# One SBUF tensor for keys and values, swapped key slots and fewer value loads at the end of a decode block

## The chip, the core and the metric

The kernel runs on one core of a Trainium2 chip. The metric is device time in microseconds (us), the median of timed runs. One more execution is recorded by the hardware profiler; all rows of the trace below are from that one.

## The reference

One decode step: two sequences (B = 2), one token each, D = 448, 16 heads of 256, a cache of 8192 positions, all in 32-bit floats.

```python
q = (layernorm(x) @ wq)                      # per head: 256
scores = einsum("bhqd,bhkd->bhqk", q, k_cache) * 256 ** -0.5
p = softmax(scores)
o = einsum("bhqk,bhkd->bhqd", p, v_cache)
h = x + o.reshape(B, 1, 4096) @ wo
h2 = h + ((ln(h) @ w_gate) * (ln(h) @ w_up)) @ w_down     # F = 1792
```

## The kernel before

There are 32 queries (head times sequence, `NQ`), numbered from 0 here. The keys of a query are 8 MB: on each of 128 partitions 64 rows (`NJ`) of 256 floats. Its values are the same size. Everything is read once.

**Engines.** VectorE makes the scores: a product of keys and query in place (`tensor_mul`), then a sum along each row (`tensor_reduce`), in two parts per query of 16 and 48 rows; the last two queries (`FINE`) in four parts of 16 rows. `top` takes the maximum over the free axis; `softmax` turns it on TensorE, takes the maximum again, and lets ScalarE make the exponentials. `mix` is the weighted sum of the values on TensorE, two rows at a time into four row groups of `o_ps`; `mixed` brings the four groups together (`o_sb`, `sel`, `oT`) and multiplies with `wo` once per head.

**Buffers.** `k_sb` is a ring of 112 rows: even queries' keys lie in rows 0 to 63, odd ones' in 48 to 111 (`k_base`). The 16 rows in common are scored first, so that the next load but one may start early. `v_sb` has 64 rows for values. Small tiles that live only at the start or the end are guests in `v_sb` (`guest`, `late_guest`).

**Order.** All large loads are issued by SyncE (SP) into one queue, in program order (the loop at line 612): values of query n-1, scores of query n, keys of query n+1. `Orders` notes who reads and writes which rows, and puts semaphore waits ahead of an instruction that needs them; an SP instruction that waits holds up all loads behind it. TensorE's part for queries 0 to `LOOP` - 1 is one loop in hardware (`turns`), the rest is straight code.

**The end.** `LATE` (line 25) cuts the values of the last four queries into nine loads, each of so many rows into its own place; `None` stands for the natural place in `v_sb`:

```python
LATE = (
    ((48, None), (16, None)),
    ((32, None), (32, None)),
    ((32, None), (32, ("k", 0))),
    ((16, ("k", 32)), (32, ("v", 32)), (16, ("v", 0))),
)
```

`EARLY` = `LOOP` = 28 is the first query of these. A query's second and later pieces are loaded behind the next keys (line 627), and summed after the next softmax (`late`, lines 621 to 624). `open_sums` (line 598) copies the sum of the other heads (`acc_ps`) and opens the last two accumulators with 16 small matmuls; for query 31 it stands ahead of the last piece of the sum (lines 641 to 645). Then come `last_head`, the second layernorm (its operand for TensorE is `xr`), the gate and up projections (`project`, `q_ps`) and the down projection (`down`, `y_ps`). The weights `wg`, `wu` and `wd` are loaded into the ring (`places`, line 660), behind the last values; `wd` in four loads.

Of the kernel before, what the change touches and what calls it, by code (L numbers as in the profile page):

```python
# [7 lines left out]
ALU = mybir.AluOpType  # L8
AX = mybir.AxisListType
# [3 lines left out]
P = 128  # L13
# [5 lines left out]
OVER = HC  # L19

AHEAD = 24
FIRST = ((NJ - AHEAD, NJ), (0, NJ - AHEAD))


LATE = (
    ((48, None), (16, None)),
    ((32, None), (32, None)),
    ((32, None), (32, ("k", 0))),
    ((16, ("k", 32)), (32, ("v", 32)), (16, ("v", 0))),
)  # L30
WQ, WO = 3 * 2 * DH + DH, 2 * D
WALL = 2 * WQ + 4 * WO
# [183 lines left out]
def decode_block(nc, x, k_cache, v_cache, w, wg, wu, wd, out):  # L216
# [3 lines left out]
    def sb(name, *shape):  # L220
        return nc.alloc_sbuf_tensor(name, list(shape), F32)[:]
# [20 lines left out]
        put("PE", "transpose", out, in_, ident[:n, :n], r=(*r, "ident"), w=w, mark=mark)  # L242

    sb("align", P, ALIGN)
    k_sb = sb("k_sb", P, 2 * NJ - OVER, DH)
    v_sb = sb("v_sb", P, NJ, DH)
    w_sb = sb("w_sb", P, WALL)
    buffers = {"k": k_sb, "v": v_sb}
    v_flat = v_sb.rearrange("p j d -> p (j d)")

    def guest(name, at, rows, *shape):

        n = 1
        for k in shape:
            n *= k
        o.homes[name] = ("v", at, n)
        got = v_flat[:rows, at : at + n]
        if len(shape) > 1:
            dims = "abc"[: len(shape)]
            got = got.rearrange(f"p ({' '.join(dims)}) -> p {' '.join(dims)}", **dict(zip(dims, shape)))  # L260
        return got
# [5 lines left out]
        h, b = divmod(i, B)  # L267
        return cache[b, h].rearrange("(p j) d -> p j d", p=P)[:, lo:hi, :]

    def load_keys(name, cache, i, lo, hi, buf, at, event=None):  # L270
        o.load(
            "SP", name, buffers[buf][:, at : at + hi - lo, :], keys(cache, i, lo, hi),
            writes=[(buf, at * DH, (at + hi - lo) * DH)], event=event,
        )

    def k_base(i):
        return i % 2 * (NJ - OVER)

    def load_k(i, lo=0, hi=NJ):
        load_keys(f"d_k_{i}_{lo}", k_cache, i, lo, hi, "k", k_base(i) + lo)  # L280

    def v_parts(i):
        got, lo = [], 0
        for n, place in LATE[i - EARLY] if i >= EARLY else ((NJ, None),):
            buf, at = place or ("v", lo)
            got.append((lo, lo + n, buf, at))
            lo += n
        return got

    def load_v(i, part):  # L290
        lo, hi, buf, at = part
        load_keys(f"d_v_{i}_{lo}", v_cache, i, lo, hi, buf, at, "e_v" if i < LOOP else None)

    def load_w(name, k, lo, hi, event=None):
        o.load("SP", name, w_sb[:, lo:hi], w[k][:, lo:hi], writes=[("w", lo, hi)], event=event)
# [5 lines left out]
        return 2 * WQ + h % 4 * WO  # L301

    load_w("d_w0", 0, 0, WQ)
    for lo, hi in FIRST:
        load_k(0, lo, hi)

    ident = sb("ident", P, P)
    put("POOL", "memset", ident, 0.0, w=["ident"])
# [134 lines left out]
    def score_parts(i):  # L443
        if i == 0:
            return list(FIRST)
        at = [(k - 1) % (NJ // HC) * HC if i % 2 == 0 else k * HC for k in range(NJ // HC)]
        if i in FINE:
            return [(lo, lo + HC) for lo in at]
        return [(at[0], at[0] + HC), (at[1], at[1] + NJ - HC)]

    def scores(i, part, between=None):
        h, b = divmod(i, B)
        s, name = s_t[i % 2], f"s{i % 2}"
        lo, hi = score_parts(i)[part]
        at = k_base(i) + lo
        kt = k_sb[:, at : at + hi - lo, :]
        qk, there = kt, ("k", at * DH, (at + hi - lo) * DH)
        if i == 0 and part == 0:
            qk, there = v_sb[:, : hi - lo, :], ("v", 0, (hi - lo) * DH)
        q, slot = qs[b], q_at(h)  # L460
        here = ("k", at * DH, (at + hi - lo) * DH)
        dve(
            "tensor_mul", qk, kt, q[:, slot, :][:, None, :].to_broadcast([P, hi - lo, DH]),
            r=[here, (f"q{b}", slot, slot + 1)], w=[there],
        )
        if between is not None:
            between()
        dve("tensor_reduce", s[:, lo:hi], qk, axis=AX.X, op=ALU.add, r=[there], w=[(name, lo, hi)])

    def top(i):  # L470
        dve("tensor_reduce", m, s_t[i % 2], axis=AX.X, op=ALU.max, r=[f"s{i % 2}"], w=["m"],
# [24 lines left out]
    def mix(i, parts):  # L496
        k = other(i)
        with common(i):
            take("e_v", i, 16)
            for lo, hi, buf, at in parts:  # L500
                for t in range(lo // 2, hi // 2):
                    g, j = 32 * (t % 4), at + 2 * t - lo
                    mm(
                        o_ps[k][g : g + 2, :], p_t[k][:, 2 * t : 2 * t + 2],
                        buffers[buf][:, j : j + 2, :], t < 4, t >= NJ // 2 - 4,
                        r=[f"p{k}", (buf, j * DH, (j + 2) * DH)], w=[f"o_ps{k}"],
                        mark="PE" if t == hi // 2 - 1 else None,
                    )

# [71 lines left out]
    def group(t, q):  # L581
        return t[:, q * YW : (q + 1) * YW]

    late_at = [HC * DH]

    def late_guest(name, rows, *shape):
        got = guest(name, late_at[0], rows, *shape)
        late_at[0] += o.homes[name][2]
        assert late_at[0] <= 2 * HC * DH
        return got  # L590

    h_sb = late_guest("h_sb", B, DC * P)
# [19 lines left out]
    for n in range(NQ + 1):  # L612
        hp, at = divmod(n, 2 * B)
        parts = v_parts(n - 1) if n > 0 else []
        if n > 0:
            load_v(n - 1, parts[0])
        if n < NQ:
            scores(n, 0, (lambda: softmax(n - 1)) if n > 0 else None)
        else:
            softmax(n - 1)  # L620
        if late is not None:
            mix(n - 2, late)
            mixed(n - 2)
            late = None
        if n + 1 < NQ:
            load_k(n + 1)
        for part in parts[1:]:
            load_v(n - 1, part)
        if n % 8 == 1:
            k = n // 8 + 1  # L630
            load_w(f"d_w_{k}", k, WQ if k == H // 4 else 0, WALL, event("e_w", n))
        def norm_last():
            if n > 0:
                norm(n - 1)

        if n == NQ:
            norm_last()
        else:
            for part in range(1, len(score_parts(n))):
                scores(n, part, norm_last if part == 1 else None)  # L640
        if n == NQ:
            mix(n - 1, parts[:-1])
            open_sums()
            mix(n - 1, parts[-1:])
            mixed(n - 1)
        elif n + 1 < NQ and len(parts) > 1:
            late = parts[1:]
            mix(n - 1, parts[:1])
        elif n > 0:
            mix(n - 1, parts)  # L650
            mixed(n - 1)
        if at == 2 and hp + 1 < H // 2:
            queries(n - 1, hp + 1)
        if n < NQ:
            if n == 0:
                o.ops["PE"].append(lambda: turns())
            top(n)

    k_flat = k_sb.rearrange("p j d -> p (j d)")
    places = {"wd": 0, "wg": (NJ - OVER) * DH, "wu": (NJ - OVER) * DH + NF * D}  # L660
    wd_t, wg_t, wu_t = (k_flat[:, places[n] :][:, : NF * D] for n in ("wd", "wg", "wu"))
    for name, t, src in (("wg", wg_t, wg), ("wu", wu_t, wu)):
        for k, half in enumerate(PIECES[name]):
            o.load("SP", f"d_{name}_{k}", t[:, half], src[:, half],
                   writes=[("k", places[name] + half.start, places[name] + half.stop)])
    at = 0
    for n in DOWN:
        o.load("SP", f"d_wd_{at}", wd_t[:, at * D : (at + n) * D], wd[:, at * D : (at + n) * D],
               writes=[("k", at * D, (at + n) * D)])
        at += n  # L670

    o.load(
# [6 lines left out]

    def project(out, out_name, t, name, k, between=None):  # L680
        wide, piece = WIDE[{"wg": "B_w_gate", "wu": "B_w_up"}[name]][k], PIECES[name][k]
        here = ("k", places[name] + piece.start, places[name] + piece.stop)
        t = t[:, piece]
        for c in range(DC):
            for g in range(4):
                xs = xr[:, c]
                if c < DC - 1:
                    at = c * sum(wide) + sum(wide[:g])
                else:
                    xs = xr[:, c + g % 2]  # L690
                    at = 3 * sum(wide) + (wide[0] if g >= 2 else 0)
                mm(
                    out[32 * g : 32 * g + 32, : wide[g]], xs.rearrange("p b r -> p (b r)"),
                    t[:, at : at + wide[g]], c == 0, c == DC - 1, r=["xr", here], w=[out_name],
                    mark="PE" if c == DC - 1 and g == 3 else None,
                )
            if c == 1 and between is not None:
                between()
# [54 lines left out]
    def down(lo, hi):  # L753
        for k in range(lo, hi):
            n, g = FF[k]
            for q in range(YN):
                mm(
                    y_ps[32 * q : 32 * q + 32, :], hmT[n // 2][:, n % 2, g, :],
                    wd_t[:, k * D + q * YW : k * D + (q + 1) * YW], False, k == NF - 1,
                    r=[f"hmT{n // 2}", ("k", k * D, (k + 1) * D)], w=["y_ps"],  # L760
                    mark="PE" if k == NF - 1 and q == YN - 1 else None,
                )

# [94 lines left out]
```

## Time and profile before

| | |
|---|---|
| median of 3 timed runs | 1301.37 us (1301.36 to 1301.38) |
| profiled execution, first to last instruction (span) | 1300.5 us |
| VectorE busy | 1130.8 us, 87% |
| TensorE matmuls busy | 488.8 us, 38% |
| ScalarE busy | 62.6 us, 5% |
| DMA: bytes read, mean rate | 561.19 MB, 432 GB/s |

The page gives no other time of the profiled execution than its span; the timed runs lie 0.87 us above it, which is what comes ahead of the first and behind the last instruction. Busy shares are averages over the whole span and say little about its end. Matmuls of 32-bit operands are done in two passes, so the trace counts twice as many as the program has; the rows that show the order of the program count each once.

### The profile page before, as it was taken

The page shows a single profiled execution, that of the slowest core. Times are in us where ns is not written, and L with a number is a line of the kernel's source. Part 1 is how long each engine was busy: PE and PEld are TensorE (multiplying, and loading weights), DVE is VectorE, ACT ScalarE, POOL GpSimd, SP SyncE. Part 2 cuts the span into 40 slices and gives each one's busy share as a digit, 9 for nine tenths or more (in the row PEclk, how much of TensorE's full clock was granted, in tenths as well). Part 3 has the DMA queues.
Part 4 walks back from the last instruction along what each step waited for, and adds up shares of the span by engine and source line. Part 5 has one row for each costly group of instructions (what it writes and reads, how often), then busy time and mean ns, then how long its engine had stood idle before and what let it go on. Part 6 is the DMA issues. An engine that isn't in the chain of part 4 may idle for free.

```text
span 1300.5 us, 6955 instructions
## 1 busy us (share of the span) xinstructions
PE 488.8 (38%) x2972; PEld 168.9 (13%) x2972; DVE 1130.8 (87%) x275; ACT 62.6 (5%) x184; POOL 1.4 (0%) x9
## 2 busy tenths in 40 slices
PE   3035422363331633215343063432424334243368
PEld 2011100120100201002101021010111001010113
DVE  7996988888988689888889868898888897889991
ACT  1000000000000000000000000000000000000000
POOL 0000000000000000000000000000000000000000
PEclk8566756686656766558666576665766667666578
DMA  9999999999999999999999999999999999999998
GB/s 414 423 434 448 424 437 431 427 441 423 448 424 435 448 423 443 427 439 429 435 435 423 433 448 423 448 424 443 427 443 427 423 436 445 426 438 429 435 433 374
DMA packets 12111, 561.45 MB, mean 432 GB/s; under 512 B 1602, under 2 KB 1732, under 8 KB 1988
## 3 DMA queue, kind: packets, MB, share of 16 engines
q1 hardware_dynamic: 12096, 561.30, 99.8%
q8 instruction: 6, 0.10, 0.0%
q14 instruction: 5, 0.04, 0.0%
q10 hardware_dynamic: 4, 0.00, 0.0%
HBM read 561.19 MB, written 0.11 MB: 432 GB/s over the span
## 4 chain that ended last, share of the span: by engine, by line
DMA 70%; DVE 29%; PE 0%; issue 0%; SPq 0%
DMA k_sb<-in_A_k_cache_dram 68%; DVE k_sb L229 14%; DVE s L229 14%; DMA k_sb<-in_wd_dram 2%; DVE nm L229 0%; PE y_ps L229 0%; SPq L176 0%; DVE m L229 0%; PE sm L229 0%; DVE v_sb L229 0%; DVE rl L229 0%
## 5 line engine op out<-in xcount | busy, mean ns | idle before, releaser
L229 DVE TENSOR_TENSOR k_sb<-k_sb,q 128x12288 f32<-128x12288 f32 (+2 forms) x67 | 549.6, 8203 | 130.3 <-DMA k_sb<-in_A_k_cache_dram 130.3
L229 DVE TENSOR_REDUCE s<-k_sb 128x48 f32<-128x12288 f32 (+2 forms) x67 | 549.3, 8198 | 0.2
L229 PE MATMUL o_ps<-v_sb,p 128*2 128x512 f32 x2000 | 288.2, 739 | 397.7 <-PEq L183 387.6
L229 PEld LDWEIGHTS o_ps<-v_sb,p 128*2 128x2 f32 x2000 | 53.7, 97 | 603.8 <-issue 591.3
L229 PE MATMUL sm<-nm,ones 1*128 1x1 f32 x64 | 16.6, 326 | 191.7 <-PEq L183 175.1
L229 PE MATMUL sm<-ident,m 128*1 128x128 f32 x32 | 10.9, 341 | 137.0 <-PEq L183 106.1
L229 PE MATMUL q_ps<-w_sb,xb 128*128 128x256 f32 (+1 forms) x172 | 59.3, 503 | 0.0
L229 ACT ACTIVATE o_sb<-o_ps 128x512 f32<-128x512 f32 x32 | 19.1, 597 | 703.9 <-PE o_ps L229 703.9
L229 PE MATMUL sm<-sel,o_sb 128*128 128x1 f32 x256 | 33.7, 253 | 25.8 <-PEq L183 22.9
L229 PE MATMUL acc_ps<-w_sb,oT 128*2 128x448 f32 x60 | 36.6, 749 | 15.9 <-PEq L183 11.0
L229 PEld LDWEIGHTS sm<-nm,ones 1*128 1x128 f32 x64 | 14.6, 283 | 201.2 <-issue 183.5
L229 PEld LDWEIGHTS sm<-sel,o_sb 128*128 128x128 f32 x256 | 31.8, 195 | 55.6 <-issue 48.2
L229 PEld LDWEIGHTS q_ps<-w_sb,xb 128*128 128x128 f32 x172 | 33.7, 200 | 30.0 <-issue 27.6
L229 PE MATMUL sm<-lsum,ones 128*128 128x1 f32 x64 | 17.5, 342 | 26.0 <-PEq L183 23.1
L229 ACT ACTIVATE nb<-sm 128x1 f32<-128x1 f32 x32 | 5.5, 171 | 395.7 <-PE sm L229 395.7
L229 PEld LDWEIGHTS sm<-ident,m 128*1 128x1 f32 x32 | 2.6, 81 | 149.8 <-issue 115.3
L229 PEld LDWEIGHTS sm<-lsum,ones 128*128 128x128 f32 x64 | 15.6, 303 | 28.0 <-issue 24.7
L229 ACT ACTIVATE q<-q_ps,rstd 128x512 f32<-128x512 f32 (+1 forms) x18 | 11.5, 640 | 71.9 <-PE q_ps L229 71.9
L229 PE MATMUL o_ps<-k_sb,p 128*2 128x512 f32 x48 | 9.3, 934 | 6.1 <-DMA k_sb<-in_A_v_cache_dram 6.1
L229 ACT ACTIVATE p<-s,nb 128x64 f32<-128x64 f32 x32 | 11.1, 347 | 1.0
L229 DVE TENSOR_TENSOR v_sb<-k_sb,q 128x6144 f32<-128x6144 f32 x1 | 6.6, 6557 | 4.8 <-DMA k_sb<-in_A_k_cache_dram 4.8
L229 PE MATMUL q_ps<-k_sb,xr 128*32 128x256 f32 (+3 forms) x96 | 10.0, 506 | 1.6 <-DMA k_sb<-in_B_w_gate_dram 1.6
(79 smaller groups left out, 85.1 us busy)
## 6 DMA issues: line engine op xcount, KB each, us to landing
v_sb<-in_A_v_cache_dram SPq DMA_DIRECT2D x4, 4096.0 KB, 30.5
w_sb<-in_w_dram SPq DMA_DIRECT2D x3, 3584.0 KB, 37.8
v_sb<-in_A_v_cache_dram SPq DMA_DIRECT2D x1, 6144.0 KB, 24.3
k_sb<-in_A_k_cache_dram SPq DMA_DIRECT2D x1, 5120.0 KB, 24.6
v_sb<-in_A_v_cache_dram SPq DMA_DIRECT2D x2, 2048.0 KB, 27.3
k_sb<-in_A_v_cache_dram SPq DMA_DIRECT2D x1, 4096.0 KB, 35.3
k_sb<-in_B_w_gate_dram SPq DMA_DIRECT2D x1, 3136.0 KB, 32.4
k_sb<-in_A_k_cache_dram SPq DMA_DIRECT2D x1, 3072.0 KB, 11.6
```

The costliest lines, as they stand in the source:

```text
L229: o.put(engine, lambda: f(*args, **kw), r, w, mark, event)
```

## The change

`k_sb` and `v_sb` become one tensor `c_sb` of 112 + 64 rows, and `RING` = 112 is the row at which the values' place begins. Even queries' keys now lie in the upper slot (rows 48 to 111), odd ones' in the lower. Query 0's first piece is its first 24 rows, loaded into the values' place and multiplied there. `LATE` has three entries: query 28 is an ordinary one, its values one load, its sum in TensorE's loop (`LOOP` = 29). A place in `LATE` is now a row of `c_sb`, so that a load may reach across the end of the ring. `wg` and `wu` lie at the ring's start, `wd` from row 84.

```diff
-FIRST = ((NJ - AHEAD, NJ), (0, NJ - AHEAD))
+FIRST = ((0, AHEAD), (AHEAD, NJ))
+RING = 2 * NJ - OVER
 LATE = (
-    ((48, None), (16, None)),
-    ((32, None), (32, None)),
-    ((32, None), (32, ("k", 0))),
-    ((16, ("k", 32)), (32, ("v", 32)), (16, ("v", 0))),
+    ((32, RING), (32, RING + 32)),
+    ((64, NJ),),
+    ((46, RING + 16), (18, NJ)),
 )
...
-    k_sb = sb("k_sb", P, 2 * NJ - OVER, DH)
-    v_sb = sb("v_sb", P, NJ, DH)
+    c_sb = sb("c_sb", P, RING + NJ, DH)
+    v_sb = c_sb[:, RING:, :]
...
     def k_base(i):
-        return i % 2 * (NJ - OVER)
+        return (1 - i % 2) * (NJ - OVER)
...
-    for lo, hi in FIRST:
-        load_k(0, lo, hi)
+    load_keys("d_k_first", k_cache, 0, *FIRST[0], RING)
+    load_k(0, *FIRST[1])
...
-        at = [(k - 1) % (NJ // HC) * HC if i % 2 == 0 else k * HC for k in range(NJ // HC)]
+        at = [(k - i % 2) % (NJ // HC) * HC for k in range(NJ // HC)]
...
         if n == NQ:
-            mix(n - 1, parts[:-1])
             open_sums()
-            mix(n - 1, parts[-1:])
+            mix(n - 1, parts)
             mixed(n - 1)
...
-    places = {"wd": 0, "wg": (NJ - OVER) * DH, "wu": (NJ - OVER) * DH + NF * D}
+    places = {"wg": 0, "wu": NF * D, "wd": (NJ + 20) * DH}
```

The order on SP, from the load of query 29's keys to the last values. Each row is a load into the tensor on the left of the arrow; the shape is partitions by floats (16384 is 64 rows, 4096 is 16). Before:

```order
L176 DMA k_sb<-in_A_k_cache_dram 128x16384 [waits DVE]
L176 DMA v_sb<-in_A_v_cache_dram 128x12288 [waits PE]
L176 DMA k_sb<-in_A_k_cache_dram 128x16384 [waits DVE]
L176 DMA v_sb<-in_A_v_cache_dram 128x4096
L176 DMA v_sb<-in_A_v_cache_dram 128x8192 [waits PE]
L176 DMA k_sb<-in_A_k_cache_dram 128x16384 [waits DVE]
L176 DMA v_sb<-in_A_v_cache_dram 128x8192 [waits PE] x2
L176 DMA k_sb<-in_A_v_cache_dram 128x8192 [waits DVE]
L176 DMA k_sb<-in_A_v_cache_dram 128x4096 [waits DVE]
L176 DMA v_sb<-in_A_v_cache_dram 128x8192 [waits PE]
L176 DMA v_sb<-in_A_v_cache_dram 128x4096 [waits PE]
```

And the same stretch now:

```order
L176 DMA c_sb<-in_A_k_cache_dram 128x16384 [waits DVE]
L176 DMA c_sb<-in_A_v_cache_dram 128x16384 [waits PE]
L176 DMA c_sb<-in_A_k_cache_dram 128x16384 [waits DVE]
L176 DMA c_sb<-in_A_v_cache_dram 128x8192 [waits PE]
L176 DMA c_sb<-in_A_k_cache_dram 128x16384 [waits DVE]
L176 DMA c_sb<-in_A_v_cache_dram 128x8192
L176 DMA c_sb<-in_A_v_cache_dram 128x16384 [waits DVE,PE]
L176 DMA c_sb<-in_A_v_cache_dram 128x11776 [waits PE]
L176 DMA c_sb<-in_A_v_cache_dram 128x4608 [waits PE]
```

All 64 rows of query 28's values now stand ahead of query 30's keys (the third row), where 48 stood before; query 30's values are one load that waits for VectorE and TensorE, and query 31's are two.

The order on TensorE, from the turned maximum of query 31 to the end of its weighted sum (`p` are the exponentials, `ident` and `pair` rows are those of `open_sums`). Before:

```order
L229 MATMUL sm<-ident,m 1x128 [waits DVE]
L229 MATMUL sm<-nm,ones 128x1 [waits ACT,DVE]
L229 MATMUL sm<-lsum,ones 128x1 [waits ACT]
L229 MATMUL o_ps<-k_sb,p 2x512 [waits d_v_31_0]
L229 MATMUL o_ps<-k_sb,p 2x512 x7
L229 MATMUL o_ps<-v_sb,p 2x512 [waits d_v_31_16]
L229 MATMUL o_ps<-v_sb,p 2x512 x15
L229 MATMUL o_ps<-v_sb,ident 2x128 [waits DVE]
L229 MATMUL o_ps<-v_sb,ident 2x128 x3
L229 MATMUL y_ps<-v_sb,pair 32x112 x4
L229 MATMUL o_ps<-v_sb,p 2x512 [waits d_v_31_48]
L229 MATMUL o_ps<-v_sb,p 2x512 x7
```

And now:

```order
L229 MATMUL sm<-ident,m 1x128 [waits DVE]
L229 MATMUL sm<-nm,ones 128x1 [waits ACT,DVE]
L229 MATMUL sm<-lsum,ones 128x1 [waits ACT]
L229 MATMUL o_ps<-c_sb,ident 2x128 [waits DVE]
L229 MATMUL o_ps<-c_sb,ident 2x128 x3
L229 MATMUL y_ps<-c_sb,pair 32x112 x4
L229 MATMUL o_ps<-c_sb,p 2x512 [waits d_v_31_0]
L229 MATMUL o_ps<-c_sb,p 2x512 x22
L229 MATMUL o_ps<-c_sb,p 2x512 [waits d_v_31_46]
L229 MATMUL o_ps<-c_sb,p 2x512 x8
```

The opening matmuls moved ahead of the whole sum, and the sum has two pieces, of 46 and 18 rows.

## Rows read from the trace of the kernel before

**Rows 1.** The page: chain by engine, the large queue, bytes.

```profile
DMA 70%; DVE 29%; PE 0%; issue 0%; SPq 0%
...
q1 hardware_dynamic: 12096, 561.30, 99.8%
...
HBM read 561.19 MB, written 0.11 MB: 432 GB/s over the span
```

**Rows 2.** The chain of waits in order of time: start us, us, what.

```profile
401.99 4.43 DVE k_sb L229
...
449.11 4.43 DVE k_sb L229
...
487.74 4.42 DVE k_sb L229
```

**Rows 3.** Timeline of SP: issues of query 30's and 31's keys, last store.

```profile
1168.39 0.33 SPq L176 DMA_DIRECT2D k_sb<-in_A_k_cache_dram  x1
...
1203.34 0.33 SPq L176 DMA_DIRECT2D k_sb<-in_A_k_cache_dram  x1
...
1298.87 0.34 SPq L176 DMA_DIRECT2D out_dram<-v_sb  x1
```

**Rows 4.** Timeline of VectorE at the end: start, us, operation, [idle before <-releaser].

```profile
1159.42 4.43 DVE L229 TENSOR_TENSOR k_sb<-k_sb,q 128x4096 f32<-128x4096 f32 x1 [3.58 <-DMA k_sb<-in_A_k_cache_dram]
...
1194.38 4.42 DVE L229 TENSOR_TENSOR k_sb<-k_sb,q 128x4096 f32<-128x4096 f32 x1
...
1203.24 4.40 DVE L229 TENSOR_TENSOR k_sb<-k_sb,q 128x4096 f32<-128x4096 f32 x1
...
1265.16 0.22 DVE L229 TENSOR_REDUCE m<-s 128x1 f32<-128x64 f32 x1
...
1268.20 0.72 DVE L229 COPY v_sb<-acc_ps 2x448 f32<-2x448 f32 x2
```

**Rows 5.** Timeline of TensorE: weighted sums of 64, 64, 32, 32 and 16 rows.

```profile
1101.58 9.83 PE L229 MATMUL o_ps<-v_sb,p 128*2 128x512 f32 x64 [12.74 <-PEq L183]
...
1140.22 9.29 PE L229 MATMUL o_ps<-v_sb,p 128*2 128x512 f32 x64 [12.73 <-PEq L183]
...
1207.80 6.20 PE L229 MATMUL o_ps<-v_sb,p 128*2 128x512 f32 x32 [0.75 <-DMA v_sb<-in_A_v_cache_dram]
...
1246.59 3.61 PE L229 MATMUL o_ps<-v_sb,p 128*2 128x512 f32 x32 [0.57 <-DMA v_sb<-in_A_v_cache_dram]
...
1268.01 3.40 PE L229 MATMUL o_ps<-k_sb,p 128*2 128x512 f32 x16
```

**Rows 6.** Timeline of what follows the last weighted sum.

```profile
1277.59 0.60 ACT L229 ACTIVATE o_sb<-o_ps 128x512 f32<-128x512 f32 x1 [10.15 <-PE o_ps L229]
...
1281.57 0.57 DVE L229 COPY xr<-sm 128x96 f32<-128x96 f32 x3 [0.74 <-PE sm L229]
...
1283.13 3.63 PE L229 MATMUL q_ps<-k_sb,xr 128*32 128x512 f32 x16 [1.60 <-DMA k_sb<-in_B_w_gate_dram]
...
1295.17 0.59 PE L229 MATMUL y_ps<-k_sb,v_sb 128*32 128x112 f32 x16
...
1296.47 2.03 PE L229 MATMUL y_ps<-k_sb,v_sb 128*32 128x112 f32 x64 [0.71 <-DMA k_sb<-in_wd_dram]
1298.10 0.16 PEld L229 LDWEIGHTS y_ps<-k_sb,v_sb 128*32 128x32 f32 x8 [0.22 <-DMA k_sb<-in_wd_dram]
```

**Rows 7.** Windows: stretch, length, busy by engine, granted clock (PEclk), DMA share, GB/s.

```profile
1282.00:1288.00 6.00, 4.87 (x24) 1.85 (x28) 1.44 (x9) 0.00 (x0) 0.00 (x0) 0.50 0.98 413
1288.00:1296.00 8.00, 7.75 (x148) 4.88 (x140) 1.86 (x5) 0.69 (x1) 0.00 (x0) 0.99 1.00 421
```

More of the change, by code (lines that the diff above doesn't have):

```diff
@@ L244, in decode_block @@
     sb("align", P, ALIGN)
-    k_sb = sb("k_sb", P, 2 * NJ - OVER, DH)
-    v_sb = sb("v_sb", P, NJ, DH)
+    c_sb = sb("c_sb", P, RING + NJ, DH)
+    v_sb = c_sb[:, RING:, :]
     w_sb = sb("w_sb", P, WALL)
-    buffers = {"k": k_sb, "v": v_sb}
-    v_flat = v_sb.rearrange("p j d -> p (j d)")
+    c_flat = c_sb.rearrange("p j d -> p (j d)")
     def guest(name, at, rows, *shape):
@@ L255, in guest @@
             n *= k
-        o.homes[name] = ("v", at, n)
-        got = v_flat[:rows, at : at + n]
+        at += RING * DH
+        o.homes[name] = ("c", at, n)
+        got = c_flat[:rows, at : at + n]
         if len(shape) > 1:
@@ L268, in keys, with rows, load_keys @@
         return cache[b, h].rearrange("(p j) d -> p j d", p=P)[:, lo:hi, :]
-    def load_keys(name, cache, i, lo, hi, buf, at, event=None):
+    def rows(at, n):
+        return ("c", at * DH, (at + n) * DH)
+    def load_keys(name, cache, i, lo, hi, at, event=None):
         o.load(
-            "SP", name, buffers[buf][:, at : at + hi - lo, :], keys(cache, i, lo, hi),
-            writes=[(buf, at * DH, (at + hi - lo) * DH)], event=event,
+            "SP", name, c_sb[:, at : at + hi - lo, :], keys(cache, i, lo, hi),
+            writes=[rows(at, hi - lo)], event=event,
         )
     def k_base(i):
-        return i % 2 * (NJ - OVER)
+        return (1 - i % 2) * (NJ - OVER)
     def load_k(i, lo=0, hi=NJ):
-        load_keys(f"d_k_{i}_{lo}", k_cache, i, lo, hi, "k", k_base(i) + lo)
+        load_keys(f"d_k_{i}_{lo}", k_cache, i, lo, hi, k_base(i) + lo)
     def v_parts(i):
         got, lo = [], 0
-        for n, place in LATE[i - EARLY] if i >= EARLY else ((NJ, None),):
-            buf, at = place or ("v", lo)
-            got.append((lo, lo + n, buf, at))
+        for n, at in LATE[i - EARLY] if i >= EARLY else ((NJ, RING),):
+            got.append((lo, lo + n, at))
             lo += n
@@ L290, in load_v @@
     def load_v(i, part):
-        lo, hi, buf, at = part
-        load_keys(f"d_v_{i}_{lo}", v_cache, i, lo, hi, buf, at, "e_v" if i < LOOP else None)
+        lo, hi, at = part
+        load_keys(f"d_v_{i}_{lo}", v_cache, i, lo, hi, at, "e_v" if i < LOOP else None)
     def load_w(name, k, lo, hi, event=None):
@@ L454, in scores @@
         lo, hi = score_parts(i)[part]
[L455 to L459, printed above, removed]
+        at = RING if i == 0 and part == 0 else k_base(i) + lo
+        kt, here = c_sb[:, at : at + hi - lo, :], rows(at, hi - lo)
         q, slot = qs[b], q_at(h)
-        here = ("k", at * DH, (at + hi - lo) * DH)
         dve(
-            "tensor_mul", qk, kt, q[:, slot, :][:, None, :].to_broadcast([P, hi - lo, DH]),
-            r=[here, (f"q{b}", slot, slot + 1)], w=[there],
+            "tensor_mul", kt, kt, q[:, slot, :][:, None, :].to_broadcast([P, hi - lo, DH]),
+            r=[here, (f"q{b}", slot, slot + 1)], w=[here],
         )
@@ L467, in scores @@
             between()
-        dve("tensor_reduce", s[:, lo:hi], qk, axis=AX.X, op=ALU.add, r=[there], w=[(name, lo, hi)])
+        dve("tensor_reduce", s[:, lo:hi], kt, axis=AX.X, op=ALU.add, r=[here], w=[(name, lo, hi)])
     def top(i):
@@ L499, in mix @@
             take("e_v", i, 16)
-            for lo, hi, buf, at in parts:
+            for lo, hi, at in parts:
                 for t in range(lo // 2, hi // 2):
@@ L504, in mix @@
                         o_ps[k][g : g + 2, :], p_t[k][:, 2 * t : 2 * t + 2],
-                        buffers[buf][:, j : j + 2, :], t < 4, t >= NJ // 2 - 4,
-                        r=[f"p{k}", (buf, j * DH, (j + 2) * DH)], w=[f"o_ps{k}"],
+                        c_sb[:, j : j + 2, :], t < 4, t >= NJ // 2 - 4,
+                        r=[f"p{k}", rows(j, 2)], w=[f"o_ps{k}"],
                         mark="PE" if t == hi // 2 - 1 else None,
@@ L582, in group @@
         return t[:, q * YW : (q + 1) * YW]
-    late_at = [HC * DH]
+    late_at = [0]
     def late_guest(name, rows, *shape):
@@ L588, in late_guest @@
         late_at[0] += o.homes[name][2]
-        assert late_at[0] <= 2 * HC * DH
+        assert late_at[0] <= HC * DH
         return got
@@ L657, in decode_block @@
             top(n)
-    k_flat = k_sb.rearrange("p j d -> p (j d)")
-    places = {"wd": 0, "wg": (NJ - OVER) * DH, "wu": (NJ - OVER) * DH + NF * D}
-    wd_t, wg_t, wu_t = (k_flat[:, places[n] :][:, : NF * D] for n in ("wd", "wg", "wu"))
+    places = {"wg": 0, "wu": NF * D, "wd": (NJ + 20) * DH}
+    wd_t, wg_t, wu_t = (c_flat[:, places[n] :][:, : NF * D] for n in ("wd", "wg", "wu"))
     for name, t, src in (("wg", wg_t, wg), ("wu", wu_t, wu)):
@@ L664, in decode_block @@
             o.load("SP", f"d_{name}_{k}", t[:, half], src[:, half],
-                   writes=[("k", places[name] + half.start, places[name] + half.stop)])
+                   writes=[("c", places[name] + half.start, places[name] + half.stop)])
     at = 0
@@ L668, in decode_block @@
         o.load("SP", f"d_wd_{at}", wd_t[:, at * D : (at + n) * D], wd[:, at * D : (at + n) * D],
-               writes=[("k", at * D, (at + n) * D)])
+               writes=[("c", places["wd"] + at * D, places["wd"] + (at + n) * D)])
         at += n
@@ L681, in project @@
         wide, piece = WIDE[{"wg": "B_w_gate", "wu": "B_w_up"}[name]][k], PIECES[name][k]
-        here = ("k", places[name] + piece.start, places[name] + piece.stop)
+        here = ("c", places[name] + piece.start, places[name] + piece.stop)
         t = t[:, piece]
@@ L759, in down @@
                     wd_t[:, k * D + q * YW : k * D + (q + 1) * YW], False, k == NF - 1,
-                    r=[f"hmT{n // 2}", ("k", k * D, (k + 1) * D)], w=["y_ps"],
+                    r=[f"hmT{n // 2}", ("c", places["wd"] + k * D, places["wd"] + (k + 1) * D)],
+                    w=["y_ps"],
                     mark="PE" if k == NF - 1 and q == YN - 1 else None,
```

## The prediction

> **What bounds the kernel now.** I read the page first. One hardware queue holds the 16 DMA engines 99.8% of the span, for 561 MB read, and 70% of the chain of waits is DMA [rows 1]. So the first question about any edit is whether it changes bytes, leaves the queue empty, or lengthens what follows the last load.
>
> Then I read the chain by time. While it runs evenly, the wait for one query's keys ends 38.63 us after the wait for those before (449.11 to 487.74 [rows 2]). In that time one load of keys and one of values pass, 64 rows a partition each: 19.32 us a load, 0.302 us a row. I use this ruler below to place landings that the trace does not show.
>
> Last I read the end, engine by engine. Until 1159.42 VectorE waits for keys [rows 4]. After that nothing holds it up: the scores of queries 29, 30 and 31 run back to back to the maximum at 1265.16 [rows 4]. From there softmax, weighted sum, projection and feed-forward follow each other on TensorE. That second chain runs beside the DMA chain: TensorE waits 1.60 us before the gate matmuls (the part of it that is the load's is about 1, since their operand xr is ready at 1282.14), 0.71 us and again 0.22 us for the down weights; the last matmul ends at 1298.50 [rows 6]. The DMA chain sets the end, but TensorE's chain is only about 0.8 us behind after 1283. **That margin is what this change must not spend.**
>
> **The change, part by part.**
>
> *One tensor, slots swapped, first piece of query 0 in the values' place.* The order of loads and the shapes on VectorE stay. The load of query 1's keys no longer waits for the first product, but it joins a queue that never emptied. Price: 0, covered by loads in flight.
>
> *Three loads fewer.* What a load costs beside its bytes can be read from the weights. A period with one more load of 3584 KB takes 47.12 us (401.99 to 449.11 [rows 2]), 8.49 us more than 38.63. The ruler gives 8.45 us for those bytes (two loads of 8192 KB in 38.63 us). What is left is 0.04 us, so three loads give back 0.1 us. The bounds are 0 and 4.8 us: the last store, alone in the queue, lasts 1.6 us from issue at 1298.87 to the end of the span at 1300.5 [rows 3], times three. I take 0.1, because every load here has another before it, as in [rows 2]. The Trainium skill, page "DMA: Bandwidth & Descriptors", section "Anatomy of one DMA", gives a fixed part of about 2.0 us per DMA, measured on the other issuing path; by it three loads would be worth an estimated 6 us. Where loads queue, this trace shows 0.04 us instead.
>
> *Query 28 whole, in the loop.* The 16 rows that used to come behind query 30's keys now come ahead of them. Before, those keys had landed by 1159.42 + 48 x 0.302 + 19.32 = 1193.2, ahead of VectorE, which took them at 1194.38 [rows 4]. Now they land at 1159.42 + 38.63 = 1198.05. VectorE waits there, and with it all that is queued behind on it. The delay is 1198.05 - 1194.38 = **3.7 us**, and nothing gives it back: query 31's keys are there in time, and the two queries' scores fill 70.8 us without a gap (1194.38 to 1265.16). The maximum of query 31 moves to 1268.8. The loop itself costs nothing: a 64-row sum takes 9.3 to 9.8 us in it [rows 5], and PE is idle afterwards until the next maximum.
>
> *The load of query 31's keys* needs the first 16 rows of query 30 scored: 8.96 us after VectorE starts (1194.38 to the issue at 1203.34 [rows 3, 4]), now 1207.0. The load ahead of it, the first half of query 29's values, still lands at 1198.05 + 9.66 = 1207.7 (before, its sum started at 1207.80 [rows 5]). The queue thus holds 0.7 us of work when the next load is issued, where it held 4.4. The hole is between 0 and 1.6 us, the whole life of that lone store; I take 0.5, near the store's time less the 0.7 still in flight. Behind it on SP stand all later loads, so every later landing moves by 0.5.
>
> *Query 30's values in one load* wait on SP for all of query 30's scores, at about 1233.4; the queue then still holds the second half of query 29's values, until about 1237.3, so no hole. They land at about 1256.5. Their 64 rows are summed by 1266.3 at the latest (9.8 us), and PE is through with the query about 2 us later, before the maximum of query 31. The 18-row load behind waits for that sum, with the 46-row load in the queue until 1270.4: no hole. The weights queue behind these, the last by 1272, also ahead of need.
>
> *The end of TensorE's chain.* Before, the sum of query 31 started 2.85 us after the maximum (1268.01 [rows 5]), and was fed in pieces as its values landed. Now the copies of the open sums and their 16 small matmuls stand ahead of the whole sum. The copies began 3.04 us after the maximum and take 0.72 [rows 4], the matmuls about 0.8: the sum starts at about 1273.3. All but the last 18 rows are there, and those land by 1276. So 64 rows run in one piece: at best 7.2 us (twice 32 rows at the high clock, 3.61 [rows 5]), at worst the loop's 9.8. I take 9.0, because they start at 1.2 GHz: 3 us at that level make 14 rows (3.40 us for 16 [rows 5]) and 50 rows at the other make 5.6, and the loop's rows lie at 9.3 and more. They end at 1282.3, not just before 1277.59.
>
> From there to the end of xr took 4.55 us (1277.59 to 1281.57 + 0.57 [rows 6]). So the gate matmuls start at 1286.9 instead of 1283.13, **3.8 us late**. From that start to the last matmul the trace has 15.4 us, of which 0.8 was waiting for the down weights, which then no longer happens. The first 5 us of it run at a granted clock of 0.50, the rest at 0.99 [rows 7]; with the gap ahead shorter by a microsecond I take off 0.3.
>
> **Sum:** 3.8 - 0.8 - 0.3 = +2.7 us. The DMA chain alone would move by 0.5 - 0.1 = +0.4 and is covered by it. The profiled span is 1300.5 us, 0.87 below the median of the timed runs; I add to the median: 1301.37 + 2.7 = **1304.1 us**.
>
> **Rivals.**
>
> *A, the forecast:* TensorE's chain becomes the bound. Its bounds: sum in 8.2 us and a better clock, 1302.9; sum in 9.8 and no clock gain, hole as taken, 1305.4. What a run on this kernel can tell from no change is about 0.2%, 2.6 us, so the line at 1303.97 cuts A nearly in half. Chance 0.66, of which 0.42 above the line.
>
> *B, not slower:* the clock pays the delay back. If the uninterrupted sum runs at 2.4 GHz almost throughout (7.2 us), and the gate matmuls too (their 5 us at 0.50 would lose up to half), 1.8 + 2.2 us come off and the last weights set the end again: 1301.8. It decides once more than 2.3 us are saved. For it: the sum at 1246.59 ran at the high level from its first row [rows 5]. Against: the two stretches that followed sparse work, at 1268.01 and 1283.13, did not [rows 5, 7]. The Trainium skill, "TensorE: Matmul & The Clock Gate", section "HAM oscillation", says that an idle gap returns TensorE to its low level; the trace agrees. Chance 0.22.
>
> *C, faster:* each load does cost a store's 1.6 us, and three give 4.8 back: 1296.6. Against it the 0.04 us of [rows 2]. Chance 0.04. By the fixed part of the Trainium skill's page named above ("DMA: Bandwidth & Descriptors", "Anatomy of one DMA") this rival would come to an estimated 1295.4.
>
> *D, worse:* the hole at query 31's keys is over about 1.5 us. Then query 30's values land so late that their one sum, ahead of query 31's maximum on TensorE, holds up the softmax as well. At a hole of 3 us this adds 1.5 to A: 1305.6, and up to 1307. Against it: the store's 1.6 us in all. Chance 0.08.
>
> **Numbers.** Faster: C, 0.04. Slower by over 0.2%: 0.42 of A and D, 0.50. Within: the rest of A and B, 0.46. The range leaves out C, the lowest of B and the end of D: 1301.5 to 1305.8. The forecast's own is 1302.9 to 1305.4.
>
> **What would show it.** Right: VectorE's first product of query 30 starts near 1198, after a wait for keys; the maximum of query 31 near 1268.8; the gate matmuls near 1287 without a wait for their weights; no wait for down weights in the last 10 us; the chain of waits runs through VectorE and TensorE from 1198 on. Wrong: a maximum of query 31 near 1265 (the keys were not late), a last sum over 9.8 or under 8 us, or TensorE still waiting for down weights at the end.

## The result, and the profile after

The changed kernel takes 1304.67 us (median of 9, 1304.53 to 1305.45) against 1301.36 us (9 runs): a ratio of 1.0025, 95% interval [1.0017, 1.0034]. It is slower, by 3.3 us where 2.7 was forecast. The way there was only half the one forecast: two chains are late at the end, not one, and in the profiled execution the other one ends last.

The profiled execution has a span of 1302.9 us, 2.4 more than the 1300.5 shown before. The other eight executions have spans of 1303.2 to 1304.0, so this span is the shortest (its time, 1304.94, is not). The span shown before is on the long side: beside the experiments the kernel before mostly had 1300.0. I use the profiles for places and causes, and the medians for prices.

The page of the changed kernel, the lines that answer to [rows 1]: chain by engine, the large queue, bytes.

```profile
DMA 72%; DVE 27%; issue 0%; PE 0%; SPq 0%
...
q1 hardware_dynamic: 11664, 561.30, 99.6%
...
HBM read 561.19 MB, written 0.11 MB: 431 GB/s over the span
```

The bytes are the same; the queue's share fell from 99.8% to 99.6%. Two tenths of a per cent of 1303 us are 2.6 us, so this small, rounded digit is a first hint that somewhere the queue stood idle.

Timeline of SP in the changed kernel (start us, us, what), answering to [rows 3]: issue of query 30's keys, of query 31's, of the four value loads behind, of the last store.

```profile
1167.96 0.33 SPq L176 DMA_DIRECT2D c_sb<-in_A_k_cache_dram  x1
...
1206.59 0.33 SPq L176 DMA_DIRECT2D c_sb<-in_A_k_cache_dram  x1
1206.96 60.17 SPq L176 DMA_DIRECT2D c_sb<-in_A_v_cache_dram  x4
...
1301.35 0.34 SPq L176 DMA_DIRECT2D out_dram<-c_sb  x1
```

Timeline of VectorE in the changed kernel, answering to [rows 4].

```profile
1197.62 4.43 DVE L229 TENSOR_TENSOR c_sb<-c_sb,q 128x4096 f32<-128x4096 f32 x1 [3.58 <-DMA c_sb<-in_A_k_cache_dram]
...
1268.41 0.22 DVE L229 TENSOR_REDUCE m<-s 128x1 f32<-128x64 f32 x1
```

VectorE now waits 3.58 us for query 30's keys, where it had none of that wait before, and the maximum of query 31 comes at 1268.41 instead of 1265.16: 3.25 us later.

Timeline of TensorE and ScalarE in the changed kernel from the sum of query 30 on, answering to [rows 5, 6].

```profile
1257.43 9.30 PE L229 MATMUL o_ps<-c_sb,p 128*2 128x512 f32 x64 [6.68 <-DMA c_sb<-in_A_v_cache_dram]
...
1272.51 8.59 PE L229 MATMUL o_ps<-c_sb,p 128*2 128x512 f32 x64 [0.21 <-DMA c_sb<-in_A_v_cache_dram]
...
1285.75 3.51 PE L229 MATMUL q_ps<-c_sb,xr 128*32 128x512 f32 x16 [0.67 <-DVE xr L229]
...
1296.27 0.97 PE L229 MATMUL y_ps<-c_sb 128*32 128x112 f32 x32 [0.48 <-DMA c_sb<-in_wd_dram]
...
1297.54 0.59 PE L229 MATMUL y_ps<-c_sb 128*32 128x112 f32 x16
...
1298.85 2.13 PE L229 MATMUL y_ps<-c_sb 128*32 128x112 f32 x64 [0.72 <-DMA c_sb<-in_wd_dram]
...
1300.58 0.16 PEld L229 LDWEIGHTS y_ps<-c_sb 128*32 128x32 f32 x8 [0.21 <-DMA c_sb<-in_wd_dram]
```

The gate matmuls start 2.62 us later (1285.75 against 1283.13) and no longer wait for their weights: that far the forecast holds. But at 1296.27, 1298.85 and 1300.58 TensorE waits for down weights; before, it did so at 1296.47 and 1298.10. The weights themselves are 2.5 us late. The forecast had them late by 0.4.

Windows of one microsecond give a hint where. The columns are those of [rows 7]; the last two are DMA share and GB/s. A packet (the piece that one DMA engine moves at a time) counts whole in the window in which it starts, which is why shares over 1 occur. First the changed kernel, then the kernel before, at the same time of the span.

```profile
1204.00:1205.00 1.00, 0.18 (x1) 0.10 (x1) 1.00 (x1) 0.00 (x0) 0.00 (x0) 0.50 1.21 524
1205.00:1206.00 1.00, 0.00 (x0) 0.00 (x0) 1.00 (x1) 0.00 (x0) 0.00 (x0) 0.50 0.31 131
1206.00:1207.00 1.00, 0.00 (x0) 0.00 (x0) 1.00 (x2) 0.00 (x0) 0.00 (x0) 0.50 0.00 0
1207.00:1208.00 1.00, 0.70 (x4) 0.11 (x8) 1.00 (x1) 0.00 (x0) 0.00 (x0) 0.50 3.17 1049
```

```profile
1205.00:1206.00 1.00, 0.82 (x4) 0.82 (x5) 1.00 (x1) 0.13 (x1) 0.00 (x0) 0.50 1.06 459
1206.00:1207.00 1.00, 1.00 (x5) 0.96 (x5) 1.00 (x1) 0.00 (x0) 0.00 (x0) 0.50 1.21 524
```

In the changed kernel no packet starts through 1206, around the issue of query 31's keys at 1206.59. By itself that proves little, because a packet here lasts 1.2 or 2.4 us and an engine can be busy with one that started earlier. The same trace has the start and the length of every packet, and they settle it. Each load is shared out over the sixteen DMA engines. On the load ahead (the first half of query 29's values) they finish one after another from 1205.4 to 1207.0. None is busy from 1207.0 to 1207.5, and the first packets of query 31's keys start at 1207.53, 0.94 us after their issue. Before, all sixteen are busy throughout. Averaged over the engines, 1.85 us are lost; and the sixteen first packets behind the hole take 3.17 us on average instead of 2.42, which adds 0.75. So the queue loses 2.6 us here.

So two theories stand against each other. **T** is the forecast's: the late chain on VectorE and TensorE sets the end. **H**: the queue ran empty at the issue of query 31's keys, and that sets the end. **L**, a third: the common tensor or the swapped slots cost something throughout.

### The profile page after: what moved, and what is told of

The parts are those of the page before. It is cut to its first block, busy times and chain, and to the rows that moved or that the text cites. A ratio compares the mean times of both kernels' runs of the same rounds, so it can differ in the third digit from the quotient of the medians.

```text
span 1302.9 us, 6967 instructions
## 1 busy us (share of the span) xinstructions
PE 484.2 (37%) x2972; PEld 167.8 (13%) x2972; DVE 1130.9 (87%) x275; ACT 62.6 (5%) x184; POOL 1.4 (0%) x9
## 3 DMA queue, kind: packets, MB, share of 16 engines
q1 hardware_dynamic: 11664, 561.30, 99.6%
## 4 chain that ended last, share of the span: by engine, by line
DMA 72%; DVE 27%; issue 0%; PE 0%; SPq 0%
DMA c_sb<-in_A_k_cache_dram 70%; DVE c_sb L229 13%; DVE s L229 13%; DMA c_sb<-in_wd_dram 2%; DVE nm L229 0%; PE y_ps L229 0%; SPq L176 0%; DVE m L229 0%; DVE rl L229 0%
## 5 line engine op out<-in xcount | busy, mean ns | idle before, releaser
L229 DVE TENSOR_TENSOR c_sb<-c_sb,q 128x4096 f32<-128x4096 f32 (+1 forms) x68 | 556.1, 8179 | 138.3 <-DMA c_sb<-in_A_k_cache_dram 138.1
L229 DVE TENSOR_REDUCE s<-c_sb 128x16 f32<-128x4096 f32 (+1 forms) x68 | 555.8, 8174 | 0.2
L229 PE MATMUL o_ps<-c_sb,p 128*2 128x512 f32 x2048 | 296.3, 743 | 410.0 <-PEq L183 400.0
L229 PEld LDWEIGHTS o_ps<-c_sb,p 128*2 128x2 f32 x2048 | 55.3, 97 | 624.5 <-issue 612.5
L229 ACT ACTIVATE oT<-sm,rl 128x2 f32<-128x2 f32 x32 | 8.4, 262 | 38.4 <-PE sm L229 38.4
L229 PE MATMUL q_ps<-c_sb,xr 128*32 128x256 f32 (+3 forms) x96 | 9.4, 481 | 0.7 <-DVE xr L229 0.7
```

What stands on the lines that cost most here:

```text
L229: o.put(engine, lambda: f(*args, **kw), r, w, mark, event)
```

## The experiments

All times are medians of several executions; "before" ran beside them each time and took 1301.41 to 1301.49 us.

**What costs nothing: the layout (e4).** The common tensor and the swapped slots, but the nine loads of before at mirrored places; the opening matmuls and the small tiles are back as before too.

```diff
-    ((32, RING), (32, RING + 32)),
-    ((64, NJ),),
-    ((46, RING + 16), (18, NJ)),
+    ((48, RING), (16, RING + 48)),
+    ((32, RING), (32, RING + 32)),
+    ((32, RING), (32, NJ)),
+    ((16, NJ + 32), (32, RING + 32), (16, RING)),
...
```

> The changed kernel's tensor, slots and first piece of query 0, but the values of the last four queries in the nine loads of the kernel before, at the mirrored places, query 28 out of the loop, opening matmuls and small tiles as before. H and T: 1301.2 to 1301.5, as the kernel before. L: 1303 or more.

Measured: 1301.46 us, ratio 1.0000 [0.9991, 1.0009]. L falls.

**Query 28 cut again (e2).** One entry added to the changed kernel's table, which also takes query 28 out of the loop.

```diff
 LATE = (
+    ((48, RING), (16, RING + 48)),
     ((32, RING), (32, RING + 32)),
```

> The changed kernel with query 28's values cut again as 48 and 16 rows (and so out of TensorE's loop); queries 29 to 31 as in the changed kernel. Query 30's keys land 4.8 us earlier, VectorE is on time (maximum of query 31 near 1265), and the issue of query 31's keys has 4.4 us in flight. Both H and T expect the whole loss to go: 1301.1 to 1301.6. Theory L (the loss is in the common tensor or the swapped slots): 1304 or more.

Measured: 1301.44 us, ratio 1.0001 [0.9992, 1.0010]. The whole loss hangs on those 16 rows standing ahead of query 30's keys (that query 28 also leaves the loop here does not matter, see e6). With e4 it also prices the loads: seven value loads (e2) and nine (e4) take the same time to 0.02 us, and the 1.6 us a load of rival C are excluded.

**The loop (e6).** The changed kernel with query 28 summed in straight code, still one load.

```diff
-LOOP = EARLY
+LOOP = EARLY - 1
```

> The changed kernel with query 28 out of TensorE's loop again, its values still one load ahead of query 30's keys. If the loop costs or saves nothing (both H and T): 1304.5 to 1305.0, as the changed kernel. If taking query 28 into the loop is part of the loss: under 1304.

Measured: 1304.85 us, ratio 1.0026 [1.0015, 1.0036], as the changed kernel. The loop is free. One line of VectorE in its profile matters below:

```profile
1270.80 0.28 DVE L229 TENSOR_REDUCE nm<-sm 1x1 f32<-1x128 f32 x1 [1.97 <-PE sm L229]
```

Here query 30's values landed 1.4 us later than in the profile of the changed kernel (1258.83 against 1257.39), their sum stood ahead of the turned maximum, and VectorE waited 1.97 us for TensorE. That is rival D's mechanism. TensorE's last matmuls then run through from 1299.26 without a wait; one weight load waits 0.2 us for down weights.

**The hole closed, VectorE left late (e1).** This was to separate T from H.

```diff
-    ((32, RING), (32, RING + 32)),
+    ((48, RING), (16, RING + 48)),
```

> The changed kernel with query 29's values cut as 48 and 16 rows, not 32 and 32, so that 16 rows more (4.8 us) are in flight when query 31's keys are issued; VectorE stays as late as in the changed kernel (maximum of query 31 at about 1268.4). Theory H (the queue ran empty at the issue of query 31's keys, 1206.59, and that costs about 2.9 us): no empty stretch there, the down weights land about 2.5 us earlier, and TensorE's chain, whose own work in the changed kernel ends 0.9 us before the last weights let it, takes over: about 1303.0 us, 1.6 under the changed kernel's 1304.67. Theory T (my prediction: TensorE's late chain sets the end): nothing that matters changes, 1304.2 to 1304.7.

Measured: 1304.81 us (1302.92 to 1308.12), ratio 1.0025 [1.0016, 1.0034]. The median is T's to 0.1 us, while the queue behaves as H said; two of the eleven executions, at 1302.92 and 1303.10, have H's number. Timeline of TensorE in e1, from the last sum on:

```profile
1273.30 9.49 PE L229 MATMUL o_ps<-c_sb,p 128*2 128x512 f32 x64
...
1288.13 3.63 PE L229 MATMUL q_ps<-c_sb,xr 128*32 128x512 f32 x16 [0.66 <-DVE xr L229]
...
1299.40 2.12 PE L229 MATMUL y_ps<-c_sb 128*32 128x112 f32 x80
```

There is no wait for weights any more: the last down matmuls run through from 1299.40. The last weights landed at 1298.17, where the changed kernel had them at 1300.54. So the hole is gone, and TensorE's chain alone sets the end, at 1301.5. It follows the forecast nearly to the step: sum from 1273.3 as worked out, 9.5 us for it (9.0 forecast), gate matmuls at 1288.1 (1286.9).

The same chain came 2.4 us earlier to the gate matmuls in the profile of the changed kernel. What differs shows in the windows of that stretch, first e1, then the changed kernel (the last column but two is the granted clock):

```profile
1272.00:1283.00 11.00, 10.40 (x80) 2.19 (x80) 0.74 (x5) 0.13 (x1) 0.00 (x0) 0.71 1.00 427
```

```profile
1272.00:1283.00 11.00, 9.95 (x85) 2.66 (x76) 0.17 (x1) 0.68 (x2) 0.00 (x0) 0.84 1.03 436
```

The mean granted clock was 0.71 in e1 and 0.84 in the changed kernel: there the sum of query 30 ended only at 1266.73 (1265.51 in e1), and TensorE was still at the high level (1.00 from 1264 to 1272, against 0.75) when softmax and the opening matmuls came. The values of query 31, late because of the hole, held the sum up by only 0.21 us. Whether the hole helps the clock in this way is not shown. Other profiles speak against a fixed link: from 1272 to 1283 the clock was 0.71 in e6, which has the hole, and 0.83 in e8 below, which has not.

**The opening matmuls back inside the sum: with the hole (e3) and without (e8).**

```diff
-            open_sums()
-            mix(n - 1, parts)
+            mix(n - 1, parts[:-1])
+            open_sums()
+            mix(n - 1, parts[-1:])
```

> The changed kernel with the opening matmuls back between the 46-row and the 18-row part of query 31's sum, so that the sum starts up to 0.8 us earlier where its values have landed. T: TensorE's chain is shorter by up to 0.8 us and so is the time, about 1304.0. H: the first 46 rows land only at 1272.5 and the down weights set the end, so no change: 1304.6 to 1304.8.

Measured: 1304.79 us, ratio 1.0026 [1.0016, 1.0037]: no gain, the number H gave. But its trace is not H's alone. The sum starts at 1272.52, when its values land, no earlier than in the changed kernel. The opening matmuls, which filled that wait before, now stand inside the sum; it ends at 1282.64 instead of 1281.10, and the last down matmuls run from 1299.55 to 1301.67 without a wait for weights, 0.7 us behind the end they have in the changed kernel. With the hole, then, the two chains end within about a microsecond and a half of each other, and either can be last, as e6 showed too; e3 does not decide between T and H.

> The kernel of e1 (no hole at query 31's keys, VectorE late, 1304.81) with the opening matmuls back between the 46-row and the 18-row part of query 31's sum. With the hole closed TensorE's chain stands alone at the end, so what is taken out of it must show: the sum may start 0.8 to 1.4 us earlier, 1303.4 to 1304.2. If something else than TensorE's chain sets the end of e1: 1304.6 to 1305.0.

Measured, on e1: 1304.11 us (1302.59 to 1304.64), ratio 1.0018 [1.0009, 1.0027]. The median is 0.7 us under e1's, within the expectation, but the two intervals overlap. Both kernels' executions fall into two groups: e1 has 2 near 1303.0 and 8 near 1304.8 (and one at 1308.12), e8 has 5 near 1302.8 and 6 near 1304.2. Group against group, e8 is 0.2 and 0.6 us shorter; the rest of the 0.7 is that more of its executions lie in the short group. Timeline of TensorE in e8's profiled execution (1302.94 us, one of the short ones; e1's is of the long group):

```profile
1271.37 7.50 PE L229 MATMUL o_ps<-c_sb,p 128*2 128x512 f32 x46
...
1286.65 3.27 PE L229 MATMUL q_ps<-c_sb,xr 128*32 128x512 f32 x16 [0.67 <-DVE xr L229]
...
1297.47 2.19 PE L229 MATMUL y_ps<-c_sb 128*32 128x112 f32 x80
```

The sum starts 1.9 us earlier than in e1, right after the exponentials, and the gate matmuls 1.5 us earlier, part of which is the clock (0.83 against 0.71 from 1272 to 1283). Again nothing waits for weights at the end. Without the hole TensorE's chain alone holds the end, and of what is taken out of it a little shows in the time.

**The hole alone (e7).** The kernel of e2, with the load of query 31's keys held back by a further piece of query 30's scores.

```diff
+GAP, MORE = NQ - 2, 7
...
+        if i == GAP:
+            return [(0, HC), (HC, HC + MORE), (HC + MORE, 2 * HC), (2 * HC, 3 * HC), (3 * HC, NJ)]
...
+                    load_k(n + 1, after=[(f"s{n % 2}", HC, HC + MORE)])
...
```

> The kernel of e2 (no loss, 1301.44) with one thing made late on purpose: query 30's scores are cut as 16, 7, 9, 16 and 16 rows, and the load of query 31's keys (with the rest of query 29's values behind it) waits for the 7-row part too, so that it is issued about 0.7 us before the load ahead of it lands, as in the changed kernel, while VectorE and TensorE are on time. The hole alone. H: it costs what it cost the DMA queue in the changed kernel, 2.5 to 2.9 us: 1303.9 to 1304.4, TensorE waiting for down weights at the end. T: the hole is small, 0.5 us: 1301.7 to 1302.2.

Measured: 1305.22 us, ratio 1.0029 [1.0018, 1.0040]; 3.8 us over e2, more than H expected, and far from T's. The hole is somewhat larger than in the changed kernel: by the packets, 2.3 us of idle engines and 0.6 for slower first packets, 2.9 in all. Timeline of VectorE and TensorE in e7:

```profile
1259.00 8.90 PE L231 MATMUL o_ps<-c_sb,p 128*2 128x512 f32 x64 [8.13 <-DMA c_sb<-in_A_v_cache_dram]
1265.01 0.22 DVE L231 TENSOR_REDUCE m<-s 128x1 f32<-128x64 f32 x1
1269.85 0.28 DVE L231 TENSOR_REDUCE nm<-sm 1x1 f32<-1x128 f32 x1 [4.62 <-PE sm L231]
...
1299.75 1.98 PE L231 MATMUL y_ps<-c_sb 128*32 128x112 f32 x64 [0.74 <-DMA c_sb<-in_wd_dram]
```

VectorE has its maximum on time at 1265.01, but then waits 4.62 us for TensorE, which is busy with query 30's 64 rows: their one load landed late, at 1259, and its sum stands ahead of the turned maximum. That is the mechanism of rival D, at work where VectorE is on time. In spite of it TensorE waits for down weights at the end, so the queue's loss sets the time.

**The hole in the middle of the run (e5).** The kernel before, one period, the load of query 14's keys held back by 18, 14 or 10 rows of scores; everything else waits for keys there, so the queue's loss is the time's.

```diff
+GAP, MORE = 13, 18
...
+        if i == GAP:
+            return [(0, HC), (HC, HC + MORE), (HC + MORE, NJ)]
...
+                    load_k(n + 1, after=[(f"s{n % 2}", HC, HC + MORE)])
```

> The kernel before with one hole in the middle: query 13's scores are cut as 16, 18 and 30 rows, and the load of query 14's keys waits for the 18-row part too, so that it is issued about 18.8 us after query 13's keys were taken, 0.5 us before the values in flight have landed. There VectorE and TensorE wait for keys in every period, so all that the queue loses shows in the time. H: 2.5 to 3.0 us, 1304.0 to 1304.5. If a hole costs no more than the life of the lone store less what is in flight: at most 1.1 us, 1301.9 to 1302.6.

> The same with 14 rows for 18: the load of query 14's keys is issued about 2.7 us before the values in flight have landed. H does not say where the loss begins; since 4.4 us in flight cost nothing in the kernel before, and 0.66 us cost 2.5 to 2.9 in the changed one, between 0 and 1.2 us: 1301.4 to 1302.6. If the loss were in the cutting of the scores and not in the queue, it would be as large as with 18 rows.

> The hole in the middle of the kernel before, with 10 rows for 18: the load of query 14's keys is issued about 4.8 us before the values in flight have landed, and everything else is as with 18 and 14 rows. The loss goes with what is in flight (3.5 us of time at 0.5 us, 1.5 at 2.6) and should be gone: 1301.3 to 1301.7. If the cut of query 13's scores costs by itself: 1302.5 or more.

| rows held back | issue of the load, us | ahead of the landing in flight, us | time, us | ratio |
|---|---|---|---|---|
| 18 | 544.73 | 0.5 | 1304.93 | 1.0027 [1.0017, 1.0037] |
| 14 | 542.47 | 2.6 | 1302.93 | 1.0012 [1.0003, 1.0021] |
| 10 | 540.41 | 4.8 | 1301.42 | 1.0000 [0.9991, 1.0009] |

(The third column is the start of VectorE's product on query 13's keys, 525.8 to 525.9, plus 19.32 us, less the issue.) The cut of the scores costs nothing (10 rows); the loss is 3.5, 1.5 and 0.0 us. Windows of e5 with 18 rows, around its issue at 544.73:

```profile
543.00:544.00 1.00, 0.00 (x0) 0.00 (x0) 1.00 (x1) 0.00 (x0) 0.00 (x0) 0.50 0.01 0
544.00:545.00 1.00, 0.00 (x0) 0.00 (x0) 1.00 (x2) 0.00 (x0) 0.00 (x0) 0.50 0.00 0
545.00:546.00 1.00, 0.68 (x4) 0.14 (x8) 1.00 (x1) 0.00 (x0) 0.00 (x0) 0.50 1.76 590
```

And the chain of waits of the same run (start us, us, what), the first product on three queries' keys:

```profile
525.91 4.42 DVE k_sb L230
...
566.59 4.42 DVE k_sb L230
...
605.23 4.42 DVE k_sb L230
```

The packets say what "0.5 us ahead of the landing" is worth. All sixteen engines are busy until 543.2; then they finish their shares of the load ahead, and the sixteen reports of its landing come between 543.53 and 545.19. The load counts as landed with the last of them. The first packet of the next load starts at 545.69, 0.96 us after its issue. So most engines had nothing to do for 2 us or more: averaged over all, 2.3 us are lost, and first packets of 3.0 us instead of 2.4 bring it to 2.9. With 14 rows the engines idle only 0.2 us, but the first packets take 2.9 us, 0.7 in all; with 10 rows nothing measurable is lost.

The next keys come 40.68 us after those before (525.91 to 566.59), not 38.63: VectorE sees 2.05 us at once, and the period after is again 38.64. It waits for the last of the sixteen engines, and behind the hole they finish closer together (0.6 us apart, 1.7 before it), so the last is less late than the average. The average of the sixteen is 2.9 us late at once and 3.5 by query 22, which is the whole loss. With 14 rows the last is 0.1 us late (the next period is 38.74 us), the average 0.7 at once and 1.1 by query 22, of 1.5 in time. What looks like a late payment is thus mostly paid at the hole. The small rest goes with some packets of 2.5 to 2.6 us behind it; their cause stays open.

**A try at a better version (e9).** e2 with more in flight ahead of query 31's keys.

```diff
-    ((32, RING), (32, RING + 32)),
+    ((40, RING), (24, RING + 40)),
```

> A try at a version better than both: the kernel of e2 (seven value loads, 1301.44) with query 29's values cut as 40 and 24 rows, so that 6.8 us instead of 4.4 are in flight when query 31's keys are issued, and those still land when VectorE takes them. If a little is lost at 4.4 us too: 1300.6 to 1301.2. If the loss ends before 4.4 us: 1301.3 to 1301.6.

Measured: 1301.63 us, ratio 1.0000 [0.9991, 1.0009]. Nothing is gained; with 4.4 us in flight nothing was lost. None of the versions beats the kernel before: e2 equals it with two loads fewer.

## Why the prediction was right, and where it was wrong

- **Nothing for the layout, the loop and the first piece:** right (e4, e6).
- **0.1 us for three loads fewer:** nothing measurable (e2 against e4). The fixed 2.0 us per DMA that the Trainium skill, "DMA: Bandwidth & Descriptors", section "Anatomy of one DMA", states for the other issuing path does not appear where loads queue here.
- **Query 30's keys late, VectorE with them:** right. 1198.05 forecast, 1197.62 measured; the maximum of query 31 at 1268.8 and 1268.41. The 0.4 us are the whole run's: query 29's keys too were taken 0.43 us earlier than in the trace of before.
- **The hole, 0.5 us out of 0 to 1.6:** this is the step that failed. The issue and the landing were placed well (1207.0 and 1207.7; 1206.59 and about 1207.3), the price was not: the queue lost 2.6 us here and the last weights came 2.5 us late. Alone, a hole of this kind costs 3.8 us at this place (e7) and 3.5 in the middle of a run (e5). I took the lone store's 1.6 us from issue to end as the upper bound and set the 0.7 us of work in flight against it. But a load lands when the last of sixteen engines is through: twelve had reported by 1206.0, 0.6 us before the issue, so little work was left in flight. The new packets then started 0.94 us after the issue, and the first of them were slow.
- **No holes at the later loads:** right. From 1214 to 1290 the engines lose 0.1 us more than in the kernel before; e1 and e2 have the same later order and their weights land in time.
- **Query 30's sum done before query 31's maximum:** right in the profiled execution, 1266.73 for 1266.3. The margin is small, and it was used up in the profiles of e6 (1.97 us of waiting) and e7 (4.62).
- **TensorE's chain 3.8 us late at the gate matmuls, the bound of the end:** in e1, where it stands alone, 5.0 us late at the gate matmuls and 1304.81 in time; so T's mechanism is real and its price was forecast well (1304.1). In the changed kernel's profile it is 2.6 us late, at a higher clock, and the late weights end 1.4 us behind it: its own work would have been over near 1299.6, an estimate (1297.54 + 0.59 + 1.94, the last 64 matmuls without waits at the rate of 0.97 us for 32, less the 0.48 waited at 1296.27), where the last matmul ended at 1300.98. The 0.9 us in the expectation of e1 left that wait of 0.48 out. "No wait for down weights" was the sign I gave, and it was wrong.
- **Rivals.** B (the clock pays it back) did not come; C is excluded. D, the hole too large, is half true: its hole is there, its knock-on at query 31's maximum is not in the changed kernel's profile, because VectorE itself is late. In e6's profile it is. Two sums do not follow from their own terms: A's upper bound comes to 1305.2 and not 1305.4 (0.8 for the sum and 0.3 for the clock on 1304.1), and the lone store's 1.6 less the 0.7 in flight are 0.9, of which I took 0.5 without a row for it.

So the time came out 0.6 us from the forecast, for a reason that the forecast had only half. Two delays, both from 16 rows moved ahead of query 30's keys, lie side by side and cost once: TensorE's, worth 3.3 us where it stands alone (e1), and the queue's, 2.5 us at the weights in the changed kernel and 3.8 in e7. That a hole five times as large as forecast hardly moved the time is luck. The overlap is why closing the queue's alone (e1), or taking a piece of TensorE's (e3), does not change the median, and undoing their common cause (e2) gives all back.

## What to carry to other kernels

In a kernel that one queue holds full, moving a load ahead of another is not free just because the bytes are the same: ask which engine's next operand now lands later, and what that engine's result releases in the queue. Keep a load's issue clear of the landing ahead of it by at least a lead that has been seen to cost nothing (here 4.4 us; 2.6 already cost 1.5 us): the landing is that of the last engine, and the others run dry before it. When undoing one of two suspects changes nothing, look for a second chain of the same length before the first is dropped.

## What the runs showed of the hardware

- The sixteen engines that share a load finish it up to 1.7 us apart (543.53 to 545.19 in e5 with 18 rows, 1205.62 to 1207.26 in the changed kernel). The landing that others wait for is the last one's.
- The first packet of a load that finds the engines idle starts 0.94 to 0.96 us after its issue (the changed kernel, e5 with 18 and with 14 rows, e7), and the first packets take 2.9 to 3.2 us on average instead of 2.4. So to leave no engine idle a load must be issued about 2.9 us ahead of the landing in flight. This is an estimate: 1.6 between the first and the last report, 0.3 by which a report follows the end of its packet, 0.95 to the first packet. At 2.6 us the engines idled 0.2 us, at 4.8 not at all.
- A queue that is let run empty for one load costs 3.5 to 3.8 us, over twice the 1.6 us that a lone small store takes from its issue to the end of the span. Of 3.5 us with 18 rows, the engines lose 2.9 on average at the hole; VectorE, which waits for the last engine, sees only 2.05 of it in that period.
- Where TensorE's chain sets the end, the time spreads by some 2 us between executions, in two groups (1302.59 to 1303.18 and 1304.11 to 1304.64 in e8), with one execution of 1308.12 in e1; where the queue alone sets it, by 0.8 to 0.9 (e2, e4). The granted clock differed between profiles of the same stretch (0.71 to 0.84); that it makes the whole of the spread was not shown.
